# One order of its own for chunk 0 of a recurrent attention, and other PSUM banks for late scores and counts

## The chip, the cores and the metric

The kernel runs on one core of a Trainium2 chip. The metric is the device time of one execution in microseconds (us); the time before is the median of three runs.

## The reference

Three parts follow each other. The first is a recurrence over 768 steps for 4 x 8 heads of width 40, with one 40 x 40 state per head:

```
for t in range(S):
    y[:, :, t] = np.einsum('bhd,bhde->bhe', rt, state)
    Sa = np.einsum('bhde,bhe->bhd', state, at)
    state_decay = state * wt[:, :, None, :] - np.einsum('bhd,bhe->bhde', Sa, bt)
    state = state_decay + np.einsum('bhd,bhe->bhde', vt, kt)
```

The second sends each of the 3072 rows of y (320 wide) to the best of 8 experts (`argmax` of `x @ w_gate`), up to a capacity per expert counted in the order of rows, and computes `gate * (relu(x @ w1[e]) @ w2[e])` with 1024 hidden units. The third is one dense layer for all rows, `relu(x @ w_in) ** 2 @ w_out`, with 2048 hidden units.

## The kernel before, in words

The recurrence is cut into 24 chunks of 32 steps (`NC`, `C`). Within a chunk the steps are solved together: the Gram products of the decay-scaled inputs (`gram`, tile G) give a triangular matrix per head; its inverse times the inputs gives the chunk's updates. Four chunks form a group, and the inverses of a group are made together on DVE: `inv_start` transposes the four chunks' matrices into L (line 227), and `inv` works off a list of products and sums (lines 278 and 282), so many of them in each chunk as a table says (`FIRST` for chunks 0 to 3). The inverse must stand in TT before the next group's first chunk.

Per chunk, in the order in which things are needed: `scan` (DVE, lines 157 and 161, cumulated decays) and `scale` (POOL or DVE, line 185) make the scaled inputs e; `gram` (PE) and `gram_mask` (DVE to N, ACT to GM) the matrices; `block_T` (line 350) copies the inverses into TB; `solve` multiplies them with X into px (line 422), which ACT copies to lu; `u` gives pu and vu; `vu_t` transposes to vut; `state` and `state_decay` carry the state to ru, `state_t` its transpose; `scores` gives pq (line 506), which DVE masks into rq (line 514); `y` the output, which `gate_in` turns into xt. The gate of the experts runs beside this: `gate.xT`, `logits`, `choose`, `count` (pc, line 971) and `rank`, and rows are scattered to their expert's place.

PSUM: `big` gives two pairs of banks in turn; `bank(k, ...)` gives one of four single banks, and each new tile in a bank waits until the old one has been read. In before, pu lies in bank 0, px and pv in banks 1 and 3, the scores in bank 1, py and the gate's products in bank 2, counts in bank 2 or, for late batches, 3, and filler matmuls (`warm`), whose result nobody reads, in bank 3.

Each engine works its own instructions strictly in the order of the program text, and the text is written out by hand in `run`. The first group's inverse is special: `inv_blocks` makes only the two 16 x 16 diagonal blocks, and `join(c)` makes the block between them for chunk c by two rounds of small matmuls on PE (jl, line 329, and jr, line 333), with a copy jm by ACT between and four copies into TT behind. Join 0 and 1 stand ahead of chunk 0, join 2 and 3 inside it, each ahead of the Gram product of a later chunk:

```
            self.block_T(c + 1)
            if c == 0:
                self.join(2)
                self.gram(5)
                self.gram_mask(5)
                self.scale(6, (V, G, V))
```

After the attention the experts and the dense layer follow on PE (lines 1428 to 1454).

Of the kernel before, what the change touches and what calls it, by code (L numbers as in the profile page):

```python
# [9 lines left out]
F32 = mybir.dt.float32  # L10
# [11 lines left out]
NC = S // C  # L22
# [13 lines left out]
class Attention:  # L36
# [280 lines left out]
        self.nat = nat.rearrange("p (a s) -> p a s", s=16)  # L317
        V.transpose(self.nat.rearrange("p a s -> p s a"), self.Tt[:, 0:16])

    def join(self, c, copies=None):  # L320

        A, T = self.nc.scalar, self.nc.tensor
        blocks = range(8 * c, 8 * c + 8)
        groups = [slice(32 * g, 32 * g + 32) for g in range(4)]
        p1, p2 = self.bank(0, f"jl{c}"), self.bank(2, f"jr{c}")
        m = self.p2.tile([128, 512], F32, tag="prod", name=f"jm{c}", bufs=3)[:, 0:128]
        for k, a in enumerate(blocks):
            for s in groups:
                T.matmul(p1[s, 16 * k : 16 * k + 16], self.GM[s, a], self.TT[s, a, 16:32], start=True, stop=True)
        A.copy(m, p1[:, 0:128])  # L330
        for k, a in enumerate(blocks):
            for s in groups:
                T.matmul(p2[s.start : s.start + 16, 16 * k : 16 * k + 16], self.nat[s, a], m[s, 16 * k : 16 * k + 16],
                         start=True, stop=True)
        for g, s in enumerate(groups):
            h = slice(s.start, s.start + 16)
            (copies[g] if copies else A.copy)(self.TT[h, 8 * c : 8 * c + 8, 16:32],
                                              p2[h, 0:128].rearrange("p (a t) -> p a t", t=16))

    def inv_end(self):  # L340
        self.nc.vector.transpose(self.TT.rearrange("p a j -> p j a"), self.Tt.rearrange("p t j -> p j t"))
# [157 lines left out]
    def scores(self, c):  # L499
        T = self.nc.tensor  # L500
        rt, vut = self.RT(c), self.vut
        pq = self.bank(1, f"pq{c}")
        for pp in range(2):
            for q in range(8):
                s = slice(64 * pp, 64 * pp + 64)
                T.matmul(pq[s, 64 * q : 64 * q + 64], vut[:, q, s], rt[:, :, q, pp], start=True, stop=True)  # L506
        self.st["q", c] = pq
# [43 lines left out]

    def run(self, extra, weights):
        LA, SHIFT = 7, 20
        EARLY, FIRST, PLAN, LAST = 1, (11, 8, 6, 2), (8, 5, 4, 2), (8, 6, 5, 0)
        V, G = self.nc.vector, self.nc.gpsimd
        gate = self.gate

# [6 lines left out]
        def wload(i):  # L564
            r = (self.L, self.Tt)[i % 2].rearrange("p a b -> p (a b)")
            weights.load(i, r[:, 0:704], 1)

        W0, W1, W2, W3 = 7, (1, 2, 2, 0), (0, 1, 0, 1, 0, 0), 0
        POOL = [(8, 1), (8, 5), (16, 1), (16, 4), (16, 7), (16, 10)]

        for c in range(4):
# [37 lines left out]
        self.inv_blocks()  # L609
        self.load(8)  # L610
        A = self.nc.scalar
        split = (A.copy, V.tensor_copy, A.copy, V.tensor_copy)
        self.scan(5)
        self.join(0, split)
        self.block_T(0, split)
        self.scale(5, (V, G, V))
        self.load_w(8)
        self.warm(W3)
        self.solve(0)
        self.join(1)  # L620
        self.gram_mask(4)
        self.scan(6)
        for c in range(6, 8):
            self.load_w(c + 3)
        idle = gate.mats.rearrange("p a b -> p (a b)")

        def chunk(c):
# [84 lines left out]
                wload(0)  # L712
                wload(1)

        def warm0(i):
            if c == 0:
                self.warm(W2[i], self.zt, 320)

        for c in range(NC - 1):
            if 1 <= c < SHIFT:  # L720
                chunk(c)
                continue
            m = c % 4
            warm0(0)
            self.u(c)
            if c == SHIFT:
                self.y(c - 1)
            bt = gate.batch(c)
            if bt:
                gate.choose(*bt)  # L730
            self.nat_k(c + 1)
            warm0(1)
            self.block_T(c + 1)
            if c == 0:
                self.join(2)
                self.gram(5)
                self.gram_mask(5)
                self.scale(6, (V, G, V))
            if m:
                self.load_r(c + 1)  # L740
            if c >= 21:
                gate.xT(c - 1)
            if c == 22:
                self.warm(1, idle, 256)
            self.state(c)
            if c:
                self.state_decay(c, None if c % 2 else V.tensor_copy)
            if c == SHIFT:
                self.gate_in(c - 1)
            if m == 0:  # L750
                self.load_r(c + 1)
                self.load(c + LA + 2, 0)
            if c == 0:
                self.scan(7)
                self.scale(7, (V, G, G))
            self.vu_t(c)
            if c == 0:
                self.state_decay(c, self.nc.scalar.copy)
            self.load(c + LA + 2, 1)
            if c == 0:  # L760
                self.join(3)
                warm0(2)
                self.gram(6)
                self.gram_mask(6)
                warm0(3)
# [7 lines left out]
            if c == 0:
                warm0(4)
                self.gram(7)
                self.gram_mask(7)
                warm0(5)
                self.inv_start(1, lambda k, h: G)
            self.solve(c + 1)
            self.load(c + LA + 2, 3)  # L780
            self.load_v(c + 2)
            if c:
                self.store_x(c - 1)
            self.scale(c + LA + 1)
            self.load_w(c + LA + 4)
            if bt:
                if c == 22:
                    self.warm(1, idle, 256)
                gate.count(*bt)
            if c:  # L790
                self.y(c)
            self.nat_n(c + 2)
            self.nat_a(c + 2)
            self.nat_pc(c + 2)
            if c == 0:
                self.block_T(2)
                self.inv("v" * FIRST[0])
            if c >= 21:
                self.gate_in(c, x22 if c == 22 else None)
            if bt:  # L800
                gate.rank(*bt)
                if c < 22:
# [61 lines left out]
class Gate:  # L864
# [99 lines left out]
    def count(self, c0, c1):  # L964

        k = c1 - c0
        self.nc.scalar.activation(self.ex[c0], self.d[c0], AF.Exp)
        pc = self.at.bank(2 if c0 < 14 else 3, f"pc{c0}")
        f = self.oh[:, c0:c1].rearrange("p b e -> p (b e)")
        for i in range(4):  # L970
            self.nc.tensor.matmul(pc[:, 32 * i : 32 * i + 8 * k], self.mats[:, i], f, start=True, stop=True)
        self.pr[c0] = self.wp.tile([128, 4, k, 8], F32, tag=f"pr{k}", name=f"pr_{c0}", bufs=2 if k == 1 else 1)
        self.nc.scalar.copy(self.pr[c0], pc[:, 0:128].rearrange("p (i b e) -> p i b e", i=4, b=4)[:, :, 0:k])
# [791 lines left out]
```

## Time and profile before

| | us |
|---|---|
| three runs | 1106.03, 1104.51, 1101.76 |
| their median | 1104.51 |
| the profiled execution's own time | 1107.43 |
| its span, first to last instruction | 1105.7 |
| PE busy | 952.9 (86%) |
| DVE busy | 733.2 (66%) |
| ACT busy | 586.3 (53%) |
| POOL busy | 305.3 (28%) |

In the rows, times are us from the span's start. Chunk 0 begins near 50, chunk 1 near 86, chunk 4 near 142; chunk 20's solve starts at 390.5, and the last scatter is issued at 479.9. PE counts a matmul in fp32 as two records, so that x64 is 32 matmuls. "[9.08 <-PE G L202]" at the end of a row is the idle time of the engine before it and what ended that.

### The profile page before, as it was taken

The page shows a single profiled execution, that of the slowest core. Times are in us where ns is not written, and L with a number is a line of the kernel's source. Part 1 is how long each engine was busy: PE and PEld are TensorE (multiplying, and loading weights), DVE is VectorE, ACT ScalarE, POOL GpSimd, SP SyncE. Part 2 cuts the span into 40 slices and gives each one's busy share as a digit, 9 for nine tenths or more (in the row PEclk, how much of TensorE's full clock was granted, in tenths as well). Part 3 has the DMA queues.
Part 4 walks back from the last instruction along what each step waited for, and adds up shares of the span by engine and source line. Part 5 has one row for each costly group of instructions (what it writes and reads, how often), then busy time and mean ns, then how long its engine had stood idle before and what let it go on. Part 6 is the DMA issues. An engine that isn't in the chain of part 4 may idle for free.

```text
span 1105.7 us, 31651 instructions
## 1 busy us (share of the span) xinstructions
PE 952.9 (86%) x13038; PEld 857.6 (78%) x13038; DVE 733.2 (66%) x1477; ACT 586.3 (53%) x1340; POOL 305.3 (28%) x439
## 2 busy tenths in 40 slices
PE   5377787787888767898989998899999999999995
PEld 3367686777778666778878998789899999999995
DVE  6848988898997935367878778867544444444432
ACT  8256576676767747335545554456534343434432
POOL 5431333262643001114545555414301010000000
PEclk6578788888988979699989999899999999999998
DMA  7845635456442323055766666434100000000000
GB/s 187 216 119 150 199 105 170 113 158 182 136 138 69 93 77 98 25 162 154 235 209 200 213 218 202 148 95 122 49 25 24 25 25 25 1 24 1 24 2 27
DMA packets 80651, 122.77 MB, mean 111 GB/s; under 512 B 9679, under 2 KB 57409, under 8 KB 79561
## 3 DMA queue, kind: packets, MB, share of 16 engines
q1 hardware_dynamic: 71173, 100.09, 31.0%
q10 hardware_dynamic: 7020, 12.78, 4.1%
q0 software_dynamic: 2304, 7.78, 2.2%
q8 instruction: 104, 1.70, 0.7%
q14 instruction: 50, 0.41, 0.1%
HBM read 91.36 MB, written 29.35 MB: 109 GB/s over the span
## 4 chain that ended last, share of the span: by engine, by line
PE 54%; DVE 23%; DMA 8%; ACT 7%; issue 5%; SPq 1%; POOL 1%; ACTq 0%; DVEq 0%; POOLq 0%
PE phg L1428 16%; PE pog L1454 5%; PE pog L1453 5%; PE pog L1452 5%; DVE pr L278 5%; PE phe L1428 4%; PE px L422 3%; PE pq L506 2%; DMA xs<-zs_s 2%; DVE rq L514 2%; DVE Tt L282 2%; DMA wB<-in_E_dram 2%; DVE e L161 1%; DMA rw<-in_w_dram 1%; PE ps L454 1%
## 5 line engine op out<-in xcount | busy, mean ns | idle before, releaser
L1438 DVE SCALAR_TENSOR_TENSOR sqg<-phg,rg 128x512 f32<-128x512 f32 x96 | 66.3, 690 | 119.0 <-ACT rg L1437 119.0
L1437 ACT ACTIVATE rg<-phg 128x512 f32<-128x512 f32 x96 | 57.2, 596 | 110.4 <-PE phg L1428 110.2
L1440 DVE TENSOR_TENSOR hlg<-sqg,hhg 128x512 fp32r<-128x512 f32 x96 | 66.5, 693 | 65.9 <-ACT hhg L1439 63.2
L1439 ACT CAST hhg<-sqg 128x512 fp32r<-128x512 f32 x96 | 59.6, 620 | 78.6 <-DVE sqg L1438 78.6
L1428 PE MATMUL phg<-xhg,e 128*128 128x512 f32 x264 | 93.1, 393 | 0.0
L422 PE MATMUL px<-TB,X 128*104 128x128 f32 x384 | 65.8, 343 | 23.5 <-DVE rq L514 13.5
L422 PEld LDWEIGHTS px<-TB,X 128*104 128x104 f32 x384 | 60.2, 225 | 26.0 <-issue 13.3
L1454 PE MATMUL pog<-e,hlg 128*128 128x320 f32 x240 | 74.1, 309 | 0.0
L1453 PE MATMUL pog<-e,hhg 128*128 128x320 f32 x240 | 74.1, 309 | 0.0
L1452 PE MATMUL pog<-e,hhg 128*128 128x320 f32 x240 | 73.9, 308 | 0.0
L185 POOL TENSOR_TENSOR e<-e 104x512 f32<-104x512 f32 x21 | 27.7, 1318 | 150.2 <-DVE e L161 56.2
L185 POOL TENSOR_TENSOR e<-e,wB 104x512 f32<-104x512 f32 x42 | 55.4, 1335 | 35.1 <-DVE wB L157 26.4
L1246 POOL TENSOR_TENSOR e<-rw,e 128x256 fp32r<-128x256 f32 x51 | 43.2, 851 | 72.3 <-ACT e L1245 69.2
L1428 PE MATMUL phe<-xhe,e 128*128 128x480 f32 (+4 forms) x176 | 58.6, 374 | 0.0
L506 PE MATMUL pq<-rq,vut 128*64 128x64 f32 x768 | 52.6, 242 | 5.7 <-issue 4.1
L1428 PEld LDWEIGHTS phg<-xhg,e 128*128 128x128 f32 x264 | 49.6, 188 | 8.8
L506 PEld LDWEIGHTS pq<-rq,vut 128*64 128x64 f32 x768 | 49.1, 154 | 7.7 <-issue 5.4
L1567 POOL DMA_INDIRECT x2g<-zs_s,idx x24 | 23.7, 989 | 113.5 <-ACT hhg L1439 105.7
L1454 PE MATMUL poe<-e,hle 128*120 128x320 f32 (+4 forms) x150 | 47.7, 318 | 7.3 <-DVE hle L1433 7.3
L1428 PE MATMUL phg<-xlg,e 128*128 128x512 f32 x132 | 51.7, 392 | 0.0
L1432 ACT ACTIVATE hhe<-phe 128x480 fp32r<-128x480 f32 (+4 forms) x64 | 33.9, 529 | 33.2 <-PE phe L1428 33.0
L514 DVE TENSOR_TENSOR rq<-pq,mQ 64x512 f32<-64x512 f32 x48 | 32.9, 685 | 21.9 <-PE pq L506 21.2
(348 smaller groups left out, 2892.6 us busy)
## 6 DMA issues: line engine op xcount, KB each, us to landing
e<-in_E_dram ACTq DMA_DIRECT2D x60, 208.0 KB
rw<-in_w_dram SPq DMA_DIRECT2D x30, 320.0 KB
zs_s<-zt SPq DMA_DIRECT2D x24, 320.0 KB
rw<-in_w_dram SPq DMA_DIRECT2D x30, 256.0 KB
e<-in_E_dram SPq DMA_DIRECT2D x9, 832.0 KB
ru<-in_VR_dram SPq DMA_DIRECT2D x48, 128.0 KB
cr<-in_wi_dram SPq DMA_DIRECT2D x20, 256.0 KB
cr<-in_wo_dram SPq DMA_DIRECT2D x20, 256.0 KB
```

Source lines behind the costliest of these rows:

```text
L185: eng.tensor_tensor(z, z, f, ALU.mult)
L278: eng.tensor_tensor(pv, in0, in1, ALU.mult)
L422: self.nc.tensor.matmul(px[par][0:104, 128 * o : 128 * o + 128], X[:, par, o, :], TB[:, 4 * par + o, :], start=True, stop=True)
L506: T.matmul(pq[s, 64 * q : 64 * q + 64], vut[:, q, s], rt[:, :, q, pp], start=True, stop=True)
L1428: T.matmul(o, lt, rt, start=(i == 0), stop=(i == len(seq) - 1))
L1437: A.activation(r[:, :n], o, AF.Relu)
L1438: V.scalar_tensor_tensor(sq[:, :n], o, 0.0, r[:, :n], ALU.max, ALU.mult)
L1439: A.copy(hh[:, :n], sq[:, :n])
L1440: V.tensor_tensor(hl[:, :n], sq[:, :n], b32(hh)[:, :n], ALU.subtract)
L1452: T.matmul(o, hh[:, t], W["h2"], start=(f == 0), stop=False)
L1453: T.matmul(o, hh[:, t], W["l2"], start=False, stop=False)
L1454: T.matmul(o, hl[:, t], W["h2"], start=False, stop=(f == NF - 1))
```

## The change

Chunk 0 leaves the common loop and gets an order of its own, written out in `run`. `join` is split: `join(c0, c1)` makes the left products of all chunks from c0 to c1 into one bank and copies them, `join_end` makes the right products and copies them into TT. Chunk 0 is joined alone, with all its copies on ACT; chunks 1 to 3 in one step. The Gram products of chunks 5 to 7 move: that of 5 right behind chunk 0's solve, that of 6 behind its state, that of 7 behind the solve of chunk 1 and ahead of chunk 1's own chain. The transpose to L stands ahead of the scan of chunk 8 and of the masks of chunk 0's scores. Two of chunk 1's block copies go to POOL, the loads for chunk 9 leave together at the end, and two filler matmuls in chunk 0 fall away. The first inversion step does twelve jobs instead of eleven in chunk 0, and seven instead of eight in chunk 1.

In all chunks from 19 on, and in chunk 0, the scores lie in bank 0 instead of 1; the counts of batches from chunk 14 on lie in bank 0 instead of 3.

```diff
-    def join(self, c, copies=None):
+    def join(self, c0, c1):
+
+        T, n = self.nc.tensor, 128 * (c1 - c0)
+        p = self.bank(0, f"jl{c0}")
+        m = self.p2.tile([128, 512], F32, tag="prod", name=f"jm{c0}", bufs=3)[:, 0:n]
+        for k, a in enumerate(range(8 * c0, 8 * c1)):
+            for g in range(4):
+                s = slice(32 * g, 32 * g + 32)
+                T.matmul(p[s, 16 * k : 16 * k + 16], self.GM[s, a], self.TT[s, a, 16:32], start=True, stop=True)
+        self.nc.scalar.copy(m, p[:, 0:n])
+        return m
+
+    def join_end(self, c0, c1, m):
...
+            self.nc.scalar.copy(self.TT[h, 8 * c0 : 8 * c1, 16:32], p[h, 0:n].rearrange("p (a t) -> p a t", t=16))
...
-        pq = self.bank(1, f"pq{c}")
+        pq = self.bank(0 if c == 0 or c >= 19 else 1, f"pq{c}")
...
-        EARLY, FIRST, PLAN, LAST = 1, (11, 8, 6, 2), (8, 5, 4, 2), (8, 6, 5, 0)
+        EARLY, FIRST, PLAN, LAST = 1, (12, 7, 6, 2), (8, 5, 4, 2), (8, 6, 5, 0)
...
-        split = (A.copy, V.tensor_copy, A.copy, V.tensor_copy)
         self.scan(5)
-        self.join(0, split)
-        self.block_T(0, split)
+        self.join_end(0, 1, self.join(0, 1))
+        self.block_T(0)
+        jm = self.join(1, 4)
         self.scale(5, (V, G, V))
         self.load_w(8)
-        self.warm(W3)
         self.solve(0)
-        self.join(1)
         self.gram_mask(4)
+        self.gram(5)
         self.scan(6)
-        for c in range(6, 8):
-            self.load_w(c + 3)
+        self.u(0)
+        self.join_end(1, 4, jm)
+        self.gram_mask(5)
+        self.scale(6, (V, G, V))
+        self.load_w(9)
+        self.vu_t(0)
+        self.nat_k(1)
+        self.block_T(1, (A.copy, G.tensor_copy, A.copy, G.tensor_copy))
+        self.load_r(1)
+        self.state(0)
+        self.gram(6)
+        self.scan(7)
+        self.gram_mask(6)
+        self.scale(7, (V, G, G))
+        self.load_w(10)
+        self.state_decay(0, A.copy)
+        self.scores(0)
+        self.solve(1)
+        self.state_t(1)
+        self.gram(7)
+        self.gram_mask(7)
+        self.inv_start(1, lambda k, h: G)
+        self.scan(8)
+        self.scores_mask(0)
+        self.scale(8)
...
+        self.inv("v" * FIRST[0])
...
-        pc = self.at.bank(2 if c0 < 14 else 3, f"pc{c0}")
+        pc = self.at.bank(2 if c0 < 14 else 0, f"pc{c0}")
```

The order of PE's instructions from the join of chunk 0 on, before (px_0 is chunk 0's solve, G_873 the Gram product of chunk 5):

```order
L329 MATMUL jl_568<-TT,GM 32x16 x32
L333 MATMUL jr_569<-jm_570,nat 16x16 x32
L422 MATMUL px_0_650<-TB_108,X_104 104x128 x4
L422 MATMUL px_0_651<-TB_108,X_104 104x128 x4
L329 MATMUL jl_662<-TT,GM 32x16 x32
L333 MATMUL jr_663<-jm_664,nat 16x16 x32
L436 MATMUL pu_747<-ru_110,lu 32x40 x32
L378 MATMUL pk_784<-ident_59,e_129 128x104 x8
L550 MATMUL warm<-zt 128x320
L329 MATMUL jl_801<-TT,GM 32x16 x32
L333 MATMUL jr_802<-jm_803,nat 16x16 x32
L202 MATMUL G_873<-e_371 32x64 x32
```

And now (G_763 is that of chunk 5):

```order
L328 MATMUL jl_568<-TT,GM 32x16 x32
L339 MATMUL jr_603<-jm_569,nat 16x16 x32
L328 MATMUL jl_644<-TT,GM 32x16 x96
L427 MATMUL px_0_748<-TB_108,X_104 104x128 x4
L427 MATMUL px_0_749<-TB_108,X_104 104x128 x4
L202 MATMUL G_763<-e_371 32x64 x32
L441 MATMUL pu_801<-ru_110,lu 32x40 x32
L339 MATMUL jr_838<-jm_645,nat 16x16 x96
```

The Gram product of chunk 5 has come forward past u(0), a transpose and two joins, and the second round of the joins comes once for three chunks, behind u(0).

DVE's order at the end of chunk 0, before (N_1088 and N_1171 are the masks of the Gram products of chunks 6 and 7, wB_647 and e_561 belong to chunk 8, rq_116 takes the masked scores of chunk 0):

```order
L185 TENSOR_TENSOR e_428<-e_428 104x512
L217 TENSOR_TENSOR N_1088<-G_1055,mN 128x256
L157 SCALAR_TENSOR_TENSOR wB_647<-wB_647,ones 104x512
L167 TENSOR_TENSOR Pc_1131<-wB_647,e_561 104x16
L169 RECIPROCAL seeds<-Pc_1131 104x16
L161 SCALAR_TENSOR_TENSOR e_561<-e_561,seeds 104x512
L514 TENSOR_TENSOR rq_116<-pq_1113,mQ 64x512 x2
L217 TENSOR_TENSOR N_1171<-G_1138,mN 128x256
L227 STREAM_TRANSPOSE L<-GM 128x32x32
L278 TENSOR_TENSOR pr_0_1218<-L,Tt 128x4
```

And now (N_1057 and N_1148 are those of chunks 6 and 7, wB_746 is chunk 8's):

```order
L217 TENSOR_TENSOR N_1057<-G_1019,mN 128x256
L185 TENSOR_TENSOR e_428<-e_428 104x512
L217 TENSOR_TENSOR N_1148<-G_1115,mN 128x256
L227 STREAM_TRANSPOSE L<-GM 128x32x32
L157 SCALAR_TENSOR_TENSOR wB_746<-wB_746,ones 104x512
L167 TENSOR_TENSOR Pc_1153<-wB_746,e_561 104x16
L169 RECIPROCAL seeds<-Pc_1153 104x16
L161 SCALAR_TENSOR_TENSOR e_561<-e_561,seeds 104x512
L519 TENSOR_TENSOR rq_116<-pq_1067,mQ 64x512 x2
L278 TENSOR_TENSOR pr_0_1193<-L,Tt 128x4
```

The transpose to L has moved ahead of the scan of chunk 8 and of the masks.

PE's order at chunk 19, with what each instruction waits for, before (pq_7157 are the scores of chunk 19, px_20 is the solve of chunk 20):

```order
L506 MATMUL pq_7157<-rq_117,vut 64x64 [waits Activation_49]
L506 MATMUL pq_7157<-rq_117,vut 64x64 x7
L422 MATMUL px_20_7176<-TB_108,X_104 104x128 [waits DVE_49,PE_49,Activation_49]
L422 MATMUL px_20_7176<-TB_108,X_104 104x128 x3
L422 MATMUL px_20_7177<-TB_108,X_104 104x128 x4
L378 MATMUL pa_7193<-ident_59,e_5018 128x104 x8
```

And now:

```order
L511 MATMUL pq_7132<-rq_117,vut 64x64 [waits Activation_49]
L511 MATMUL pq_7132<-rq_117,vut 64x64 x7
L427 MATMUL px_20_7151<-TB_108,X_104 104x128 [waits PE_49,Activation_49]
L427 MATMUL px_20_7151<-TB_108,X_104 104x128 x3
L427 MATMUL px_20_7152<-TB_108,X_104 104x128 [waits PE_49]
L427 MATMUL px_20_7152<-TB_108,X_104 104x128 x3
L383 MATMUL pa_7168<-ident_59,e_4993 128x104 x8
```

The order is the same; the solve has lost its wait for DVE and keeps those for ACT and PE.

## Rows read from the trace of the kernel before

**Rows 1.** Stretches; busy us of PE, PEld, DVE, ACT, POOL; granted clock, DMA share, GB/s.

```profile
97.00:142.00 45.00, 34.33 (x965) 30.11 (x960) 42.85 (x69) 24.58 (x60) 12.05 (x10) 0.79 0.68 199
520.00:1105.00 585.00, 551.68 (x3154) 507.03 (x3152) 340.88 (x662) 272.61 (x610) 138.98 (x165) 0.98 0.30 91
```

**Rows 2.** PE in order of time, chunk 0: start, us, instruction, idle before.

```profile
48.48 1.05 PE L329 MATMUL jl<-TT,GM 32*32 32x16 f32 x64 [9.25 <-DVE TT L341]
49.92 0.72 PE L333 MATMUL jr<-jm,nat 32*16 32x16 f32 x64 [0.39 <-ACT jm L330]
54.05 3.71 PE L422 MATMUL px<-TB,X 128*104 128x128 f32 x16 [3.41 <-DVE TB L350]
...
78.46 3.31 PE L506 MATMUL pq<-rq,vut 128*64 128x64 f32 x32
81.70 0.90 PE L202 MATMUL G<-e 64*32 64x64 f32 x64
83.35 1.97 PE L422 MATMUL px<-TB,X 128*104 128x128 f32 x16 [0.75 <-DVE rq L514]
```

**Rows 3.** Two stretches of chunk 0, columns as in rows 1.

```profile
54.00:60.00 6.00, 5.52 (x191) 5.15 (x194) 5.11 (x7) 1.72 (x5) 2.36 (x2) 0.67 0.88 272
82.00:86.00 4.00, 3.25 (x86) 2.99 (x65) 3.50 (x4) 1.60 (x4) 1.54 (x3) 1.00 0.25 64
```

**Rows 4.** ACT in order of time, chunk 0.

```profile
59.70 1.10 ACT L337 COPY TT<-jr 16x128 f32<-16x128 f32 x4 [0.82 <-PE jr L333]
...
61.10 1.69 ACT L441 COPY vu<-pu 32x320 f32<-32x320 f32 x4
62.81 1.59 ACT L411 ACTIVATE rhsY<-pk,sgn 64x640 f32<-64x640 f32 x2
64.43 1.68 ACT L350 COPY TB<-TT 32x256 f32<-32x256 f32 x4
...
84.48 0.59 ACT L425 COPY lu<-px 104x512 f32<-104x512 f32 x1 [0.40 <-PE px L422]
```

**Rows 5.** DVE in order of time, chunk 0 and the start of chunk 1.

```profile
68.33 0.42 DVE L217 TENSOR_TENSOR N<-G,mN 128x256 f32<-128x256 f32 x1 [9.08 <-PE G L202]
...
76.20 0.42 DVE L217 TENSOR_TENSOR N<-G,mN 128x256 f32<-128x256 f32 x1 [2.77 <-PE G L202]
76.54 1.21 DVE L157 TENSOR_TENSOR_SCAN wB<-wB,ones 104x512 f32<-104x512 f32 x1
...
78.30 1.23 DVE L161 TENSOR_TENSOR_SCAN e<-e,seeds 104x512 f32<-104x512 f32 x1
81.81 1.39 DVE L514 TENSOR_TENSOR rq<-pq,mQ 64x512 f32<-64x512 f32 x2 [2.28 <-PE pq L506]
...
84.11 2.14 DVE L227 STREAM_TRANSPOSE L<-GM 128x1024 f32<-128x1024 f32 x1 [0.45 <-ACT GM L219]
86.28 0.17 DVE L278 TENSOR_TENSOR pr<-L,Tt 128x4 f32<-128x4 f32 x1
...
96.02 0.42 DVE L217 TENSOR_TENSOR N<-G,mN 128x256 f32<-128x256 f32 x1 [2.81 <-ACT GM L216]
```

**Rows 6.** POOL in order of time, scalings in chunk 1.

```profile
102.96 2.47 POOL L185 TENSOR_TENSOR e<-e,wB 104x512 f32<-104x512 f32 x2 [1.16 <-DVE wB L157]
```

**Rows 7.** DVE beside those scalings.

```profile
104.20 1.69 DVE L278 TENSOR_TENSOR pr<-Xm,Tt 128x256 f32<-128x256 f32 x1
```

**Rows 8.** PE in order of time, chunks 19 to 23.

```profile
390.53 3.71 PE L422 MATMUL px<-TB,X 128*104 128x128 f32 x16 [8.06 <-DVE rq L514]
...
409.92 3.42 PE L422 MATMUL px<-TB,X 128*104 128x128 f32 x16 [1.58 <-DVE rq L514]
414.07 1.06 PE L971 MATMUL pc<-oh,mats 128*128 128x16 f32 x8 [0.73 <-ACT lu L425]
...
461.14 1.87 PE L971 MATMUL pc<-oh,mats 128*128 128x8 f32 x8 [1.13 <-ACT vut L497]
```

**Rows 9.** ACT in order of time, copies to TB for chunk 20.

```profile
383.29 1.64 ACT L350 COPY TB<-TT 32x256 f32<-32x256 f32 x4 [2.29 <-DVE ab L980]
```

More of the change, by code (lines that the diff above doesn't have):

```diff
@@ L318, in inv_blocks @@
         V.transpose(self.nat.rearrange("p a s -> p s a"), self.Tt[:, 0:16])
-    def join(self, c, copies=None):
[L322 to L333, printed above, removed]
+    def join(self, c0, c1):
[9 more added lines that the diff above has]
+    def join_end(self, c0, c1, m):
+        T, n = self.nc.tensor, 128 * (c1 - c0)
+        p = self.bank(2, f"jr{c0}")
+        for k, a in enumerate(range(8 * c0, 8 * c1)):
+            for g in range(4):
+                s = slice(32 * g, 32 * g + 32)
+                T.matmul(p[32 * g : 32 * g + 16, 16 * k : 16 * k + 16], self.nat[s, a], m[s, 16 * k : 16 * k + 16],
                          start=True, stop=True)
[L335 to L338, printed above, removed]
+        for g in range(4):
+            h = slice(32 * g, 32 * g + 16)
+            self.nc.scalar.copy(self.TT[h, 8 * c0 : 8 * c1, 16:32], p[h, 0:n].rearrange("p (a t) -> p a t", t=16))
     def inv_end(self):
@@ L566, in wload @@
             weights.load(i, r[:, 0:704], 1)
-        W0, W1, W2, W3 = 7, (1, 2, 2, 0), (0, 1, 0, 1, 0, 0), 0
+        W0, W1 = 7, (1, 2, 2, 0)
         POOL = [(8, 1), (8, 5), (16, 1), (16, 4), (16, 7), (16, 10)]
@@ L611, in run @@
         A = self.nc.scalar
-        split = (A.copy, V.tensor_copy, A.copy, V.tensor_copy)
         self.scan(5)
-        self.join(0, split)
-        self.block_T(0, split)
+        self.join_end(0, 1, self.join(0, 1))
+        self.block_T(0)
+        jm = self.join(1, 4)
         self.scale(5, (V, G, V))
         self.load_w(8)
-        self.warm(W3)
         self.solve(0)
-        self.join(1)
         self.gram_mask(4)
+        self.gram(5)
         self.scan(6)
-        for c in range(6, 8):
-            self.load_w(c + 3)
+        self.u(0)
[23 more added lines that the diff above has]
+        self.scale(8)
+        self.load(9, 0)
+        self.load(9, 1)
+        self.load(9, 2)
+        self.load(9, 3)
+        self.load_w(11)
+        self.load_v(2)
+        self.nat_n(2)
+        self.nat_a(2)
+        self.nat_pc(2)
+        self.block_T(2)
+        self.inv("v" * FIRST[0])
         idle = gate.mats.rearrange("p a b -> p (a b)")
@@ L713, in chunk @@
                 wload(1)
[L715 to L720, printed above, removed]
+        for c in range(1, NC - 1):
+            if c < SHIFT:
                 chunk(c)
@@ L723, in run @@
             m = c % 4
-            warm0(0)
             self.u(c)
@@ L731, in run @@
             self.nat_k(c + 1)
-            warm0(1)
             self.block_T(c + 1)
[L734 to L738, printed above, removed]
             if m:
@@ L745, in run @@
             self.state(c)
-            if c:
-                self.state_decay(c, None if c % 2 else V.tensor_copy)
+            self.state_decay(c, None if c % 2 else V.tensor_copy)
             if c == SHIFT:
@@ L752, in run @@
                 self.load(c + LA + 2, 0)
-            if c == 0:
-                self.scan(7)
-                self.scale(7, (V, G, G))
             self.vu_t(c)
-            if c == 0:
-                self.state_decay(c, self.nc.scalar.copy)
             self.load(c + LA + 2, 1)
[L760 to L765, printed above, removed]
             if c < 21:
@@ L772, in run @@
             self.scores_mask(c)
[L773 to L778, printed above, removed]
             self.solve(c + 1)
@@ L781, in run @@
             self.load_v(c + 2)
-            if c:
-                self.store_x(c - 1)
+            self.store_x(c - 1)
             self.scale(c + LA + 1)
@@ L789, in run @@
                 gate.count(*bt)
-            if c:
-                self.y(c)
+            self.y(c)
             self.nat_n(c + 2)
@@ L794, in run @@
             self.nat_pc(c + 2)
-            if c == 0:
-                self.block_T(2)
-                self.inv("v" * FIRST[0])
             if c >= 21:
```

## The prediction

> **What bounds the kernel now.** I read the stretches first, then each engine's instructions in order of time, and last the releasers beside the waits. In 97 to 142 us (chunks 1 to 3) DVE is busy 42.85 of 45 us [rows 1]: it works off the inversion of the second group of four chunks, and whatever lets it begin earlier moves chunk 4. From 520 us on PE is busy 551.68 of 585 us, so the second half is as long as PE's work and begins when attention ends. The two places that the change touches are bound by no engine; they are relays. In chunk 0 DVE waits 9.08 us for the Gram product of chunk 5 and 2.77 for that of chunk 6 [rows 5], PE being held up by the joins. In chunks 19 to 22 PE stands before the solve's product px until DVE has masked the scores: once 8.06 us, then three times 1.57 or 1.58 (the first is shown) [rows 8].
>
> **Chunk 0, step by step.** The join of chunk 0 ends as before on PE at 49.92 + 0.72 = 50.6 [rows 2]. All eight copies behind it are ACT's now, 1.10 + 1.68 = 2.8 us [rows 4], to 53.4, where px began at 54.05 with the copies shared. Beside them PE runs the left products of chunks 1 to 3, three times 0.8 to 1.05, to 53.8 at most. So px starts at 53.8, no later than before.
>
> Px took 3.71 there and 1.97 at 83.35; the granted clock was 0.67 in the one stretch and 1.00 (2.4 GHz) in the other [rows 2, 3]. PE now has work from 48.5 on with gaps under half a us, where it rested 3.41 before px, so I take 1.97; the other end is 3.71. The two filler matmuls that chunk 0 loses would have come later. Px ends at 55.8. Second copy to lu 0.59 [rows 4], to 56.4. On PE the Gram product of chunk 5 (0.9, as G in rows 2) and u(0) (as many matmuls, 0.9) to 57.6; vu 1.69 [rows 4], to 59.3, the right products of chunks 1 to 3 (three times 0.72) beside it and behind it. ACT then carries the relay: one set of four TT copies of 384 columns, between the 1.10 of one set of 128 and three times that (16 rows of 128 take 0.28 each and 32 of 320 take 0.42, so 0.47 each, 1.9), to 61.2; GM, as wide as N, 0.4; two copies of vut, 512 columns as lu, 1.2; rhsY 1.59 [rows 4], to 64.4. That frees the PSUM pair that chunk 6's Gram product needs. G to 65.3, DVE's N 0.4, ACT's GM 0.4, to 66.2, and the state copies to ru, as wide as rhsY's, 1.6, to 67.8. PE meanwhile does scores and px(1): half of the 3.31 [rows 2] at the full clock, 1.7, and 2.0, to 69; then pn and G of chunk 7, 0.9 each, to 70.8. N and GM 0.9: DVE's transpose to L starts at 71.7, where it started at 84.11 [rows 5].
>
> Not all of the 12.4 is gain, as two pieces of DVE that lay in its waits now stand behind that transpose: scan(8), from 76.54 to 79.53, 3.0 us, and the masks of scores(0), 1.39 [rows 5]. L 2.14, to 73.8; scan to 76.8; masks to 78.2; there the inversion begins, against 86.28. Eleven jobs took from 86.28 to where the wait before the next N begins, 96.02 - 2.81 = 93.21, so 6.9; the twelfth, drawn forward from chunk 1, is two instructions of 256 columns at 0.42, 0.9. End 86.0.
>
> Here is a price: POOL's three scalings of chunk 8, about 3.7 us by the pair in [rows 6], used to lie before the inversion and now start at 76.8 beside its first jobs. Where POOL's pair ran, a DVE product of 256 columns took 1.69 us [rows 7], 1.3 more than an N of that size [rows 5]. I charge that once, to 87.3; none and three times are the ends. The Trainium skill (GPSIMD Engine Reference, Key points) says that GpSimd shares its SBUF interfaces with VectorE and contends with its two-input instructions. By that rule every product beside the scalings is at risk, and the 87.3 would be up to 89.7; the slow product in the trace agrees with it.
>
> Scores(0) now lies in bank 0, which u(1) needs. So u(1), which PE could start at 72, waits for the masks to 78.2. Behind it on PE stand px(2), y(0), pk and G(8): 0.9 for u, then px at the slow 3.71 after a rest of 6 us, 0.9 twice, rhsY 1.59, G beside it, GM 0.4: 86.6. So N(8) comes at 87.3 from DVE's side and 86.6 from PE's, against 96.02. Gain 8.7; with one job fewer in chunk 1, of which PE must follow half, 9. The edits that I cost at nothing: POOL's two copies for chunk 1 start at 61.2 and take about 0.6 each (half of a scaling in [rows 6]), the scaling of chunk 7 behind them ends near 65, and neither is wanted before 66. Of the DMAs, the four loads of chunk 9 go out in a row on ACT behind GM(7), about 72; ACT's copies behind them have until 78, and the user, scan(9), comes after N(8). On SP's queue the loads for u(2) now stand behind a load of decay factors that waits for scale(8), so until 80.5 (76.8 + 3.7); u(2) too comes after N(8). Where a cover is gone, the price is the lateness itself.
>
> The lower end: with px(0), scores and px(1) at the slow clock, 1.7 us each, L comes at 76.8, and N(8) near 93, a gain of 3. The upper end: no charge for POOL and all of the twelfth job, 11.5.
>
> **The late scores and counts.** Chunk 19: px(20) needs ACT's TB copies, which end at 383.29 + 1.64 = 384.9 [rows 9], and banks 1 and 3. Bank 1 held the scores, whose masks stand on DVE behind ranks, state and xt; px started at 390.53. In bank 0 the scores no longer hold it: 5.6 us. The wait goes to u(20): px takes 3.7 and four small groups 0.9 each, so it comes near 392, and the masks are there at 390.5, where they let px go before. Chunks 20 to 22: px follows the scores at once, 1.58 and twice 1.57. The count of chunk 20 also waited 0.73 for the copy of bank 3 [rows 8]; it now needs only the masks, which fall under px. In chunk 22 a filler matmul in bank 3 stands before the count and waits for the same copy, so nothing there. In the last chunk the count waited 1.13 for vut; it moves up, and the scores behind it too. Sum 5.6 + 1.58 + 0.73 + 3.14 + 1.13 = 12.2 us. I count each whole, as the rows name the masks or the copy as what came last; the ends are 7 (the gain of chunk 19 and one other) and 14 (some px of 3.4 to 3.7 at the full clock, since PE no longer rests before it).
>
> Together 21.2. What a removed wait uncovers I can follow to the next engine, not further, so I take a tenth off: 19. The profiled execution took 1107.43 us, span 1105.7; 1107.4 - 19 = 1088.4. It lies 2.9 above the median of the three runs, 1104.51; so 1085.5.
>
> **Rivals.**
> The late gain alone. Chunk 0 gives 3 or less, the solves running at the slow clock and ACT carrying one relay more. For it: every TT and TB copy of chunk 0 is ACT's, and a rest of 3.4 us stands before the slow px(0). Against it: three round trips of PE and ACT for the joins of chunks 1 to 3 become one. 1104.5 - 12.2 - 1 = 1091.
>
> Chunk 0's gain alone: the masks were where the tail waited, but the ranks and scatters behind them set the end. For it: DVE has one long run of ranks at each batch. Against it: px(20) waits for the masks and for nothing of the ranks. 1104.5 - 9 = 1095.5.
>
> The change does not do what it says: what attention saves, the second half waits for, because weights or rows arrive no earlier. For it: that half loads weights throughout. Against it: its loads are issued behind attention's end and move with it. 1104.
>
> Slower: the second half gets PE at the lower clock for more of its time. Place: 520 to the end, 551.68 us of PE at a mean granted clock of 0.98 [rows 1]. Price: each hundredth costs 551.7 / 98 = 5.6 us. It decides from four hundredths on, which eat the 21 us; at 0.93 the time would be 1104.5 - 19 + 28 = 1113. For it: the clock does differ between stretches [rows 3]. Against it: the slow px(0) came after a rest of PE, and the change makes none in that half.
>
> **How the numbers follow.** Forecast as summed, 0.62, its own range 1078 to 1091 (from 11.5 + 14 down to about 6 + 8). Late gain alone 0.17 (1089 to 1095), chunk 0 alone 0.08 (1094 to 1098), nothing 0.06, slower 0.07. The range 1078 to 1096 takes nearly all of the first two and half of the third, and leaves out some 2 in 10. A measurement of this kernel tells about 0.5%, 5.5 us, from no change: faster by more than that 0.87, within it 0.06, slower 0.07.
>
> **What would show it.** In the changed profile: px(0) near 2 us and begun by 54; DVE's wait before N(5) gone, one before N(7) of some 4 us in its place; the transpose to L near 72 and u(1) released by rq, near 78; N(8) by 88; no wait of px(20) to px(23) on rq, px(20) released by TB; the first product of the second half some 20 us earlier, the granted clock there 0.98. Px(0) at 3.7, or N(8) after 92, would show chunk 0 wrong. A px(20) that waits for something new, or an unchanged gap between px(20) and the last count, would show the late sum wrong.

## The result: 1.5% faster, all of it from the late banks

| | before | changed | ratio (95% interval) |
|---|---|---|---|
| first comparison, median us | 1105.27 (4 runs) | 1088.04 (4 runs) | 0.986 [0.981, 0.990] |
| second comparison, median us | 1105.58 (21 runs) | 1087.44 (6 runs) | 0.984 [0.981, 0.987] |
| profiled execution, own time / span | 1107.43 / 1105.7 | 1085.83 / 1084.1 | |

The forecast of 1085.5 us stands 2 to 3 us from both medians. Its two terms do not: chunk 0 was to give 9 us and gave none, the late scores and counts were to give 12.2 and gave some 19 (made alone, 18.8). The sum came out right by luck: the two errors cancelled.

**Chunk 0.** PE in order of time in the changed kernel, which answers to [rows 2]. Columns: start, us, engine, line, instruction, idle before it and what ended that.

```profile
46.70 1.05 PE L328 MATMUL jl<-TT,GM 32*32 32x16 f32 x64 [8.95 <-DVE TT L346]
48.14 0.70 PE L339 MATMUL jr<-jm,nat 32*16 32x16 f32 x62 [0.39 <-ACT jm L329]
...
48.70 1.63 PE L328 MATMUL jl<-TT,GM 32*32 32x16 f32 x104
51.89 1.37 PE L328 MATMUL jl<-TT,GM 32*32 32x16 f32 x86 [1.57 <-issue]
53.19 3.74 PE L427 MATMUL px<-TB,X 128*104 128x128 f32 x16
56.86 0.51 PE L202 MATMUL G<-e 64*32 64x64 f32 x26
58.93 0.64 PE L202 MATMUL G<-e 40*32 40x64 f32 x38 [1.56 <-issue]
59.50 0.80 PE L441 MATMUL pu<-ru,lu 128*32 128x40 f32 x64
60.23 0.33 PE L339 MATMUL jr<-jm,nat 32*16 32x16 f32 x25
62.76 1.25 PE L339 MATMUL jr<-jm,nat 32*16 32x16 f32 x128 [2.19 <-issue]
67.31 0.51 PE L339 MATMUL jr<-jm,nat 32*16 32x16 f32 x39 [3.30 <-issue]
...
86.45 1.30 PE L441 MATMUL pu<-ru,lu 128*32 128x40 f32 x64 [5.54 <-DVE rq L519]
```

Four times PE stops in the middle of a series of like matmuls, waiting for nothing that the profile shows ("issue"): 1.57 + 1.56 + 2.19 + 3.30 = 8.6 us. In before, "issue" cost 0.5 us in this part of the program (44 to 98 us). Now count the records between two stops: 86 jl, 16 px and 26 G are 128; 38 G, 64 pu and 25 jr are 127; then 128 jr. The stops come every 127 or 128 matmul records, whatever the matmuls are.

Before has such stops too. The largest near chunk 0 lies just behind that part, 128 records after a small one:

```profile
97.57 1.55 PE L506 MATMUL pq<-rq,vut 128*64 128x64 f32 x27 [0.20 <-issue]
...
104.72 0.34 PE L436 MATMUL pu<-ru,lu 128*32 128x40 f32 x14 [1.79 <-issue]
```

DVE in order of time in the changed kernel, the answer to [rows 5] (N(c) is its mask of the Gram product of chunk c):

```profile
44.66 1.99 DVE L346 STREAM_TRANSPOSE TT<-Tt 128x1024 f32<-128x1024 f32 x1
...
59.61 0.42 DVE L217 TENSOR_TENSOR N<-G,mN 128x256 f32<-128x256 f32 x1 [3.17 <-PE G L202]
...
74.10 0.42 DVE L217 TENSOR_TENSOR N<-G,mN 128x256 f32<-128x256 f32 x1 [9.96 <-PE G L202]
...
79.39 0.42 DVE L217 TENSOR_TENSOR N<-G,mN 128x256 f32<-128x256 f32 x1 [4.27 <-PE G L202]
80.26 2.01 DVE L227 STREAM_TRANSPOSE L<-GM 128x1024 f32<-128x1024 f32 x1 [0.45 <-ACT GM L219]
...
86.43 0.17 DVE L278 TENSOR_TENSOR pr<-L,Tt 128x4 f32<-128x4 f32 x1
...
86.82 0.94 DVE L278 TENSOR_TENSOR pr<-L,Tt 128x16 f32<-128x16 f32 x1
...
88.00 1.00 DVE L278 TENSOR_TENSOR pr<-L,Tt 128x36 f32<-128x36 f32 x1
...
96.07 0.42 DVE L217 TENSOR_TENSOR N<-G,mN 128x256 f32<-128x256 f32 x1
```

DVE's old wait of 9.08 us for the Gram product of chunk 5 is back as 9.96 us for that of chunk 6. The transpose to L comes at 80.26 (forecast 71.7), N(8) at 96.07, where it was at 96.02 [rows 5]. The executions do not begin alike: the first group's TT transpose stands at 44.66 here and at 46.42 in before, ahead of every change. So places in chunk 0 are best told from that transpose, and the tables below do so. From it to the second group's TT transpose there are 91.94 us in before and 92.01 in the changed kernel: no gain. In five profiles with the old order (before and four of the experiments) this is 90.0 to 92.4 us, in three with the new one (the changed kernel twice, and once with the late banks put back) 91.0 to 92.7.

**The late part.** PE in the changed kernel, which answers to [rows 8]:

```profile
385.30 3.38 PE L427 MATMUL px<-TB,X 128*104 128x128 f32 x16 [2.53 <-ACT TB L355]
...
400.06 1.90 PE L511 MATMUL pq<-rq,vut 128*64 128x64 f32 x32
401.89 2.00 PE L427 MATMUL px<-TB,X 128*104 128x128 f32 x16
403.72 0.96 PE L975 MATMUL pc<-oh,mats 128*128 128x16 f32 x8
...
444.32 1.06 PE L975 MATMUL pc<-oh,mats 128*128 128x8 f32 x8
...
446.35 1.90 PE L511 MATMUL pq<-rq,vut 128*64 128x64 f32 x32
...
455.95 1.06 PE L975 MATMUL pc<-oh,mats 128*128 128x8 f32 x8
```

No px waits for rq any more, and px(20) is released by TB, as forecast. From the start of the TB copies for chunk 20 (383.29 in [rows 9], 383.61 now) to the last count (476.15 in before) it took 92.9 us and takes 72.3: 20.5 less. The waits that went are 5.5 + 4.7 + 0.7 + 1.1 and 0.3 at a late filler, 12.4 in all; two small ones came, 0.69 of "issue" and 0.29 for vu. The other 9 us are PE's own groups: px(21) took 3.42 [rows 8], now 2.00; the last chunk's count 1.87, now 1.06. The scores of chunks 20 and 23 in before, and then the stretch from px(20) to the last count, in before and in the changed kernel, there with the second half behind it (busy us of PE, PEld, DVE, ACT, POOL; granted clock, DMA share, GB/s):

```profile
405.50 2.85 PE L506 MATMUL pq<-rq,vut 128*64 128x64 f32 x32
...
464.65 3.17 PE L506 MATMUL pq<-rq,vut 128*64 128x64 f32 x32
```

```profile
390.50:477.10 86.60, 68.13 (x1369) 59.34 (x1369) 35.20 (x134) 42.96 (x112) 9.02 (x10) 0.81 0.24 72
```

```profile
385.20:456.90 71.70, 59.16 (x1367) 51.72 (x1367) 40.38 (x150) 42.75 (x113) 9.98 (x11) 0.93 0.30 85
500.00:1084.00 584.00, 553.62 (x3156) 509.23 (x3154) 340.96 (x662) 273.18 (x611) 139.26 (x166) 0.98 0.30 91
```

The granted clock over this work rose from 0.81 to 0.93, and PE's busy time fell from 68.13 to 59.16 us; busy time times clock is 55 in both, so it is the same work at another clock. Which groups are slow changes from one execution to the next, and with it the sum: this way from the TB copies to the last count is 92.9 and 92.2 us in two profiles with the old late banks, and 70.7 to 75.4, in the middle 73.6, in nine with the new ones. So 19 us is nearer to what the change gives than 20.5. The second half, 553.62 us of PE at 0.98, is what it was [rows 1], only earlier.

### The profile page after: what moved, and what is told of

Same layout as the page of the kernel before. It is cut to its first block, busy times and chain, and to the rows that moved or that the text cites. A ratio compares the mean times of both kernels' runs of the same rounds, so it can differ in the third digit from the quotient of the medians.

```text
span 1084.1 us, 31641 instructions
## 1 busy us (share of the span) xinstructions
PE 943.6 (87%) x13034; PEld 850.4 (78%) x13034; DVE 734.9 (68%) x1473; ACT 584.5 (54%) x1332; POOL 305.6 (28%) x441
## 4 chain that ended last, share of the span: by engine, by line
PE 57%; DVE 17%; ACT 6%; issue 5%; DMA 4%; POOL 2%; SPq 1%; ACTq 0%; DVEq 0%; POOLq 0%
PE phg L1432 16%; PE pog L1458 5%; PE pog L1457 5%; PE pog L1456 5%; PE phe L1432 5%; PE px L427 4%; DVE pr L278 3%; PE pq L511 2%; DMA xs<-zs_s 2%; DVE Tt L282 2%; PE poe L1458 1%; PE poe L1456 1%; PE poe L1457 1%; PE ps L459 1%; DVE rq L519 1%
## 5 line engine op out<-in xcount | busy, mean ns | idle before, releaser
L1432 PEld LDWEIGHTS phg<-xhg,e 128*128 128x128 f32 x264 | 49.6, 188 | 8.8
L1436 ACT ACTIVATE hhe<-phe 128x480 fp32r<-128x480 f32 (+4 forms) x64 | 33.9, 529 | 36.8 <-PE phe L1432 36.3
L511 PE MATMUL pq<-rq,vut 128*64 128x64 f32 x768 | 48.5, 229 | 5.6 <-issue 4.4
L511 PEld LDWEIGHTS pq<-rq,vut 128*64 128x64 f32 x768 | 44.8, 142 | 7.4 <-issue 5.8
L446 ACT COPY vu<-pu 32x320 f32<-32x320 f32 x96 | 39.9, 416 | 14.4 <-PE pu L441 13.3
```

Of the source, the lines that this page charges most:

```text
L1432: T.matmul(o, lt, rt, start=(i == 0), stop=(i == len(seq) - 1))
```

## The experiments

The reasons to be tested: (A) the whole gain is the late banks'; (B) chunk 0's order gains nothing because PE outruns the supply of its instructions; (C) the late gain is the waits plus PE's clock.

### The late banks alone, and chunk 0 alone

The first kernel is before with these two edits:

```diff
-        pq = self.bank(1, f"pq{c}")
+        pq = self.bank(0 if c >= 19 else 1, f"pq{c}")
...
-        pc = self.at.bank(2 if c0 < 14 else 3, f"pc{c0}")
+        pc = self.at.bank(2 if c0 < 14 else 0, f"pc{c0}")
```

> The kernel before, with only the late banks changed: scores of chunks 19 to 23 and counts from chunk 14 on in bank 0; chunk 0 as it was. Theory (read from the changed kernel's trace): the whole gain comes from here, 12 us of waits removed and some 8 us because PE, no longer resting, keeps its full clock; so 17 to 21 us below the kernel before. Rival (the forecast's sum): the late banks give 12 and chunk 0 the rest; 11 to 13 us below.

Measured: 1086.68 us, ratio 0.9835 [0.980, 0.987], 18.8 us under the 1105.47 of before beside it. From the TB copies to the last count 73.6 us.

The second is the changed kernel with both banks back as in before, only the scores of chunk 0 still in bank 0:

```diff
-        pq = self.bank(0 if c == 0 or c >= 19 else 1, f"pq{c}")
+        pq = self.bank(0 if c == 0 else 1, f"pq{c}")
...
-        pc = self.at.bank(2 if c0 < 14 else 0, f"pc{c0}")
+        pc = self.at.bank(2 if c0 < 14 else 3, f"pc{c0}")
```

> The changed kernel with only the late banks put back (scores of 19 to 23 in bank 1, late counts in bank 3); chunk 0 in its new order. Theory: chunk 0's new order gains nothing, within 2 us of the kernel before, since PE stands without instructions for some 8 us between 48 and 68. Rival (forecast): 9 us below; rival of the forecast's lower end: 3 below.

Measured: 1107.04 us, ratio 1.001 [0.998, 1.003]. Two lines of the change make all its gain, and the order of chunk 0 makes none: (A) holds.

### Are the rests worth more than their length?

Before, with filler matmuls where PE waits for rq: six of 256 columns ahead of px(20), two ahead of px(21) to px(23).

```diff
+                self.warm(6, idle, 256)
...
+            if c >= SHIFT:
+                self.warm(2, idle, 256)
```

> The kernel before, with filler matmuls whose result nobody reads put into PE's waits ahead of the solves of chunks 20 to 23 (six, then two each); no wait is removed. Theory (the clock): the waits remain, but the groups behind them run at the full clock as in the changed kernel, px(21) near 2.0 instead of 3.4 us and scores of chunk 22 near 1.9 to 2.7 instead of 3.3; 3 to 8 us below the kernel before. Rival (the clock does not hang on these waits): within 2 us of the kernel before.

Measured: 1104.84 us, ratio 1.0005 [0.998, 1.003]; the expected gain did not come. PE in that kernel:

```profile
407.24 2.81 PE L506 MATMUL pq<-rq,vut 128*64 128x64 f32 x32
409.98 1.13 PE L550 MATMUL warm<-mats 128*128 128x256 f32 x4
411.62 1.97 PE L422 MATMUL px<-TB,X 128*104 128x128 f32 x16 [0.52 <-DVE rq L514]
```

Px(21) is down to 1.97. That does not show that its rest had slowed it, for in the kernel with only chunk 0 changed it took as much behind the whole rest:

```profile
410.06 1.97 PE L427 MATMUL px<-TB,X 128*104 128x128 f32 x16 [1.57 <-DVE rq L519]
```

Px still may not start before rq is masked, and the scores ahead of it stay at 2.81. The fillers lie in the waits and take nothing from them. From TB to the last count it is 91.2 us, 1.7 or 1.0 less than in the two profiles with the old late banks. The fillers left 4.11 us of the first rest and 0.52 of each other one, so how PE would run without any rest is not shown by this.

### Chunk 19's scores alone, and those of chunks 20 to 23 alone

Two kernels, each before with one edit:

```diff
-        pq = self.bank(1, f"pq{c}")
+        pq = self.bank(0 if c == 19 else 1, f"pq{c}")
```

> The kernel before, with the scores of chunk 19 alone in the other bank. Theory (the late gain is the waits taken away, 12.4 us, plus some 8 us that PE's groups get shorter where its rests before px(21) to px(23) go): here only the first wait goes, 5.5 us and nothing more, so 1099.5 and ratio 0.995; px(21) and the scores' groups stay as long as before. Rival (the 8 us hang on the phase that the earlier px(20) gives): 10 us or more, ratio 0.990 or less.

```diff
-        pq = self.bank(1, f"pq{c}")
+        pq = self.bank(0 if c >= 20 else 1, f"pq{c}")
```

> The kernel before, with the scores of chunks 20 to 23 alone in the other bank; chunk 19's scores and the counts as before. Theory (the part of the late gain beyond the waits comes where PE's short rests before px(21) to px(23) go, since its groups behind them then run at the full clock): 4.7 us of waits and some 6 to 8 us of shorter groups, so near 1093.5, ratio 0.989; px(21) 2.0 us instead of 3.4, px(20) still released by rq. Rival (the waits alone): 4.7 us, 1100.5, ratio 0.9957.

Measured: 1100.08 us, 0.995 [0.993, 0.998], for chunk 19; 1098.14 us, 0.9935 [0.991, 0.996], for chunks 20 to 23. From TB to the last count:

| kernel | us | less than before | waits taken away |
|---|---|---|---|
| before | 92.9 | | |
| chunk 19's scores | 84.3 | 8.6 | 5.5 |
| scores of 20 to 23 | 85.6 | 7.2 | 4.7 |
| all late scores and counts | 73.6 | 19.2 | 12.4 |
| changed | 72.3 | 20.5 | 12.4 |

In these profiles each piece gives its waits and 2.5 to 3.1 us more, no more than two profiles of like kernels differ by; what is left, 3 to 5 us, holds the counts, whose own waits are 1.9, and whatever the pieces give only together. By the medians they give 5.0 and 7.4 us, and both intervals hold the waits alone. That px(21) would stay slow in the first was wrong: it took 1.96, although its wait of 1.58 was still there. In the second it took 2.76, not 2.0, and the 6 to 8 us that the theory put on chunks 20 to 23 did not come. So the extra is shown for all the waits together (18.8 us for 12.4); which rests it hangs on stays open.

### Is it data traffic that holds up PE's instructions?

The changed kernel with five zero-filling stores of 320 KB behind chunk 0 instead of ahead of it:

```diff
-        extra(0, 5)
...
         self.load_v(2)
+        extra(0, 5)
```

> The changed kernel with five zero fills of 320 KB, written to DRAM ahead of chunk 0, moved behind chunk 0's loads, so that the DMA queues are free from about 50 us on. Theory A (PE's instructions come late because the DMA engines are full of data): PE's stretches without work inside the joins, 8.6 us in sum, shrink to under 3, and the time falls by 3 to 6 us against the changed kernel. Theory B (PE works off many small matmuls faster than instructions come, however free the DMA is): the stretches remain at 6 us or more and the time stays within 2 us of the changed kernel's 1088.

Measured: 1091.76 us, 0.989 [0.984, 0.993]. The long stops remain: 1.84 and 0.38 before the joins' second round, 2.19 and 3.07 in it, 7.5 us against 8.6. One of the four nearly went; the supply is not set by these stores. The DMA engines were not free, though: from 52.5 to 70.4 us they were busy for 0.41 of the time, against 0.56 in the changed kernel (50 to 68 us), so other transfers are not ruled out as a part of it. The time lies 3.7 us above the changed kernel's 1088.04, where theory B said at most 2; the intervals overlap.

### Fewer small matmuls ahead of the Gram product

The changed kernel, with the right products of chunks 2 and 3 behind the Gram product of chunk 7:

```diff
-        self.join_end(1, 4, jm)
+        self.join_end(1, 2, jm[:, 0:128])
...
         self.gram_mask(7)
+        self.join_end(2, 4, jm[:, 128:384])
```

> The changed kernel, with the right products of the joins taken apart: those of chunk 1 stay behind u(0), those of chunks 2 and 3 go behind the Gram product of chunk 7. Theory (PE outruns its instructions in the long dense series of small matmuls, and the 5.5 us of gaps in jr hold up the Gram product of chunk 6): two thirds of the series and most of the 5.5 us leave the path, so N(6) comes near 68 instead of 74.10, the transpose to L near 75, N(8) some 4 us earlier, and the kernel takes 3 to 5 us less than the changed one: ratio to before near 0.982. Rival (ACT's copies set N(6), the gaps are only idle time beside them): N(6) moves by less than 1.5 us and nothing is gained: 0.986.

Measured: 1085.24 us, 0.983 [0.981, 0.985]. N(6) came 4.9 us earlier than in the changed kernel's first profile and 3.6 than in its second (table below), and L and the second group's inverse 3 to 5 earlier. The last right product ahead of the Gram product ended 4.2 us earlier than in the first profile, though only 1.25 us of matmuls had been moved away: the rest is a stop. The remaining 0.7 is ACT's copies, which are shorter; they stand in this chain, but begin only when the right products are done. PE's stops there:

```profile
60.78 0.64 PE L202 MATMUL G<-e 40*32 40x64 f32 x38 [1.41 <-issue]
61.35 0.80 PE L441 MATMUL pu<-ru,lu 128*32 128x40 f32 x64
62.08 0.33 PE L339 MATMUL jr<-jm,nat 32*16 32x16 f32 x25
64.88 0.51 PE L339 MATMUL jr<-jm,nat 32*16 32x16 f32 x39 [2.46 <-issue]
...
75.99 0.65 PE L339 MATMUL jr<-jm,nat 32*16 32x16 f32 x60
78.24 0.71 PE L339 MATMUL jr<-jm,nat 32*16 32x16 f32 x68 [1.60 <-issue]
```

### DVE's order, and both edits

The changed kernel with the scan and scalings of chunk 8 ahead of the mask of chunk 6, and the masks of scores(0) ahead of that of chunk 7:

```diff
         self.scan(7)
+        self.scan(8)
         self.gram_mask(6)
         self.scale(7, (V, G, G))
+        self.scale(8)
...
         self.gram(7)
+        self.scores_mask(0)
         self.gram_mask(7)
         self.inv_start(1, lambda k, h: G)
-        self.scan(8)
-        self.scores_mask(0)
-        self.scale(8)
```

> The changed kernel, with DVE's order altered: the scan and scalings of chunk 8 stand ahead of the mask of the Gram product of chunk 6, where DVE waited 9.96 us, and the masks of scores(0) ahead of N(7), where it waited 4.27. Theory: the inversion begins right behind the transpose to L, near 82.4 instead of 86.43, without POOL's scalings beside it (1.5 us), u(1) is released some 5 us earlier, and N(8) comes near 90.5 instead of 96.07; the second group's inverse stands 5 us earlier, ratio to before near 0.981. Rival (the chain of PE and ACT through chunk 1 sets N(8) and what follows): N(8) moves by less than 2 us, no gain: 0.986.

> Both of these edits in the changed kernel. Theory: the transpose to L near 75, the inversion at once behind it, N(8) near 86, which is the 9 to 10 us that the prediction gave to chunk 0; ratio to before near 0.977, 1080 us. Rival: the two hide one another's gain, or chunk 1 is bound by ACT and PE: N(8) at 90 or later, ratio 0.982 or more.

Measured: 1084.09 us, 0.981 [0.978, 0.984], for DVE's order alone, and 1084.32 us, 0.9805 [0.978, 0.983], for both edits. The inversion begins right behind L, and no scaling of POOL lies beside it; here in the kernel with both:

```profile
77.86 2.14 DVE L227 STREAM_TRANSPOSE L<-GM 128x1024 f32<-128x1024 f32 x1 [0.45 <-ACT GM L219]
80.03 0.17 DVE L278 TENSOR_TENSOR pr<-L,Tt 128x4 f32<-128x4 f32 x1
...
80.43 0.18 DVE L278 TENSOR_TENSOR pr<-L,Tt 128x16 f32<-128x16 f32 x1
...
92.43 0.42 DVE L217 TENSOR_TENSOR N<-G,mN 128x256 f32<-128x256 f32 x1 [4.36 <-ACT GM L216]
```

DVE's order alone brought N(8) 1.6 to 2.9 us earlier than in the two profiles of the changed kernel, near the rival's 2 and not the theory's 5.6. With both edits it came at 92.43, 46.1 us behind the first group's TT transpose, where the theory's 86 is 41.3: DVE is now done with its twelve jobs sooner, and waits 4.36 us for chunk 1's chain on PE and ACT. On PE that chain starts late:

```profile
84.87 3.74 PE L427 MATMUL px<-TB,X 128*104 128x128 f32 x16 [2.99 <-ACT TB L355]
```

These TB copies end at 84.82; ahead of them ACT issues the four loads of chunk 9 until 81.91. The rival was right that the two edits hide part of one another's gain. In us from the first group's TT transpose:

| kernel | N(6) | L | inversion | N(8) | second group's TT |
|---|---|---|---|---|---|
| before | 29.8 | 37.7 | 39.9 | 49.6 | 91.9 |
| changed | 29.4 | 35.6 | 41.8 | 51.4 | 92.0 |
| changed, once more | 28.1 | 34.2 | 40.4 | 50.1 | 91.0 |
| joins apart | 24.5 | 30.6 | 36.8 | 46.5 | 88.0 |
| DVE's order | 30.2 | 36.4 | 38.5 | 48.5 | 89.8 |
| both | 25.3 | 31.6 | 33.7 | 46.1 | 87.4 |
| 64 more small ones | 35.8 | 41.9 | 48.1 | 57.7 | 98.3 |
| two wide ones | 30.4 | 36.5 | 42.6 | 52.3 | 92.8 |

The medians of joins apart, DVE's order and both are 2 to 4 us under the changed kernel's, less than a measurement tells apart. In its profiled execution the kernel with both edits had lost its 4.6 us again by chunk 20 (TB for it at 384.38); why is open.

### More instructions, or more work?

The changed kernel with 64 more matmuls like the right products behind them, and the same with two matmuls of 256 columns in their place:

```diff
         self.join_end(1, 4, jm)
+        w = self.bank(3, "warm")
+        for k in range(16):
+            for g in range(4):
+                s = slice(32 * g, 32 * g + 32)
+                self.nc.tensor.matmul(w[32 * g : 32 * g + 16, 16 * k : 16 * k + 16], self.nat[s, 8 + k],
+                                      jm[s, 16 * k : 16 * k + 16], start=True, stop=True)
```

```diff
         self.join_end(1, 4, jm)
+        self.warm(2, gate.mats.rearrange("p a b -> p (a b)"), 256)
```

> The changed kernel with 64 more matmuls like the right products (16 columns each, result unread) behind join_end(1, 4), ahead of what leads to the Gram product of chunk 6. Their own time on PE is some 1.4 us. Theory (PE's instructions come in pieces of 128 records, of which one takes some 4 us or more to arrive): a further gap of 2.5 us or more, the Gram product of chunk 6 and N(6) 3.8 to 4.6 us later relative to the first TT transpose. Rival (the gaps have another cause, such as waits that the profile does not name): N(6) later by the 1.4 us of their own time, at most 2.

> The changed kernel with two matmuls of 256 columns (result unread) in the place of those 64 small ones: 1 to 1.9 us of PE, but only 4 records. Theory (instructions set the pace there, not PE's work): the wide ones fall into the gap before the next piece, so that N(6) moves by under 0.7 us. Rival (PE's time sets it): N(6) later by their full 1 to 1.9 us.

Measured: 1091.74 us, 0.988 [0.986, 0.991], with the small ones; 1085.94 us (two runs), 0.982 [0.977, 0.987], with the wide ones; the changed kernel beside them 1087.44. PE with the small ones:

```profile
69.08 1.24 PE L339 MATMUL jr<-jm,nat 32*16 32x16 f32 x128 [1.94 <-issue]
72.53 0.49 PE L339 MATMUL jr<-jm,nat 32*16 32x16 f32 x37 [2.21 <-issue]
...
72.88 0.94 PE L633 MATMUL warm<-jm,nat 32*16 32x16 f32 x87
75.99 0.52 PE L633 MATMUL warm<-jm,nat 32*16 32x16 f32 x39 [2.18 <-issue]
```

One more stop appears, 128 records behind the last one. It is 2.18 us, under the 2.5 expected, and N(6) is 6.3 and 7.7 us later than in the two profiles of the changed kernel, 3.0 of them because the first stop, ahead of the edit, was 4.53 this time. The 3.4 to 4.7 that are left for 64 matmuls hold the theory's 3.8 to 4.6 and not the rival's 2. From one such stop to the next it is 3.45 us, for 1.24 of work. The wide ones took 2.08 us of PE, brought no stop but one of 0.37 ahead of the Gram product, and moved N(6) by 1.0 to 2.3 us against the two profiles of the changed kernel. The theory had them hidden, under 0.7; they were not. So this pair supports the count of records, and leaves it open how far PE's work can lie beside the supply.

### The changed kernel once more

> The changed kernel once more, beside these, for a narrower ratio and to see how far its trace differs from one profiled execution to the next: 0.986 of before, issue gaps of 6.5 to 9 us in the joins in the same places, the first product of the second half some 20 us earlier.

Measured: 1087.44 us, 0.984 [0.981, 0.987]. The stops: 1.55 in jl, 3.65 and 2.48 in jr, 7.7 us; the one in G is missing, and that in jr longer for it.

## Why the prediction was right in its sum and wrong in its terms

**The step that failed in chunk 0** is "PE now has work from 48.5 on with gaps under half a us, so I take 1.97". PE rested 8.95 us before the joins and stopped for 1.57 in them, and px(0) took 3.74 at a granted clock of 0.50 (53 to 57 us). The stops came to 8.6 us in all, where the prediction had gaps of under half a us. Together that is 1.8 + 8.6 = 10.4 us; the transpose to L, taken from the first TT transpose, came 10.3 later than forecast. ACT's copies into TT show that all of this lies ahead of them:

```profile
67.87 1.95 ACT L343 COPY TT<-jr 16x384 f32<-16x384 f32 x4 [5.81 <-PE jr L339]
```

From there to L it was 12.4 us, as forecast (59.3 to 71.7). The sum has slips that decide nothing: by its own terms the right products end at 59.8, half a us behind the copies that read them; 86.0 and three times 1.3 are 89.9, not 89.7; and the terms of chunk 0's upper end add up to about 11, not 11.5.

What followed was as forecast, only later. U(1) was released by rq, after PE had stood 5.54 us. POOL's scalings beside the inversion slowed two products, from 0.18 and 0.20 to 0.94 and 1.00, together 1.6 us for the 1.3 charged. DVE waited 4.27 before N(7). The wait before N(5) did not go (3.17). By the prediction's own signs (px(0) at 3.7, N(8) after 92) the chunk 0 term was wrong, and the 3.6 to 4.9 us by which the Gram product of chunk 6 moved, when 64 small matmuls (128 records) moved behind it, show why. Leaving the scan and the masks behind L then gave away what the earlier L still had: L to inversion takes 6.2 us, 2.2 before.

The profile of before could have warned: 0.5 us of "issue" there did not mean that instructions were plentiful, but that PE's waits for ACT gave them time; the stop of 1.79 at 104.72 was there to be counted. Each of the four joins had such a wait in its middle, jr for ACT's copy jm, 5.2 us in all; the change took three of them away and put the products end to end. The Trainium skill (Runtime: NRT & Kernel Launch, section Instruction fetch mechanics) says that instructions come in blocks of 16 KiB, 256 of them, while the current block runs, and that crossing a boundary is mostly hidden. The trace agrees on the block: 128 matmul records with their 128 weight-load records stand between two stops, and queue q8 moves 16 KB in a packet (below). It does not agree on "mostly hidden" where a block of small matmuls runs in 1.24 us.

**In the late part the mechanism was right and its size wrong.** Every removed wait went, with its forecast length (12.4 for 12.2), and only 1 us came in their place. The upper end of 14 named the missing cause, "some px of 3.4 to 3.7 at the full clock, since PE no longer rests before it", and gave it 2 us; it was 6 (18.8 - 12.4, by the times) to 9 (by the two profiles shown), since not only px but scores, counts, transposes and fillers run in that stretch, whose clock was 0.81. Taking the waits away brought it; fillers in the same waits, which left part of each rest, brought no more than 1.7 us. Which rest slowed which group is not settled.

Of the rivals, "the late gain alone" described what chunk 0 gives rightly (3 us or less, the solve at the slow clock), though not PE's stops, and missed by 3 to 4 us because it took over the late term. The slower clock in the second half did not come: 0.98 as before.

## What to carry to other kernels

Joining series of small matmuls to save round trips can cost more than the trips: count the matmul records in the stretch, divide by 128, and ask whether each such piece has some 4 us of time (3.45 to 4.55 here). Where the granted clock of a stretch is well under 1, a wait of PE can cost more than its length: here 12.4 us of waits were worth some 19. And a total that comes out right proves no term: undoing one half of the change takes one run.

## What was not expected of the hardware

PE's instructions arrive in pieces, and the page of the profile shows it. Its lines on PE's records (first fence) and on the instruction queue (second), in the changed kernel:

```profile
PE 943.6 (87%) x13034; PEld 850.4 (78%) x13034; DVE 734.9 (68%) x1473; ACT 584.5 (54%) x1332; POOL 305.6 (28%) x441
```

```profile
q8 instruction: 104, 1.70, 0.7%
```

104 packets of 16.3 KB for 13034 matmul records are 125 records to a packet; with 64 matmuls (128 records) more it was 105 packets for 13162, so this queue seems to be PE's. Where PE had used up a piece early, the next series began 3.45 to 4.55 us after the last one had. In the joins that means 64 matmuls in some 4 us, however small they are.
